# Splitting the attention scores of batches 2 and 3 into three fp32r products on a Trainium2 core

## The chip, the core and the metric

One kernel runs on one core of a Trainium2 chip. A core has five engines that run side by side and wait for each other through semaphores: TensorE (PE in the rows, with its weight loads as PEld), VectorE (DVE), ScalarE (ACT), GpSimd (POOL) and SyncE (SP, which here only issues DMAs). TensorE reads SBUF and writes PSUM, which has eight banks of 128 x 512 fp32. The metric is the device time of one execution in microseconds (us).

## The reference

Three stages follow each other. Inputs q, k, v are fp32 of shape (4 batches, 8 heads, 576 positions, 64 dims); f has one decay per position.

```python
scores = (q @ k.T) / sqrt(64) + (cum[i] - cum[j])      # cum = cumsum(log(f)), causal mask
attn   = softmax(scores);  a = attn @ v                # -> x, 2304 tokens x 512
h      = x @ w_in;  g = h * tanh(softplus(h));  z = g @ w_out      # 512 -> 2048 -> 512
out    = max(z @ w1, z @ w2, z @ w3) @ w_out2                      # 512 -> 768 -> 512
```

## The kernel before

All engines get one list of instructions each. The order of every list is set ahead of time by a scheduler, which takes the program as it is written, its priorities (attention is emitted at a high priority, the first feed-forward product `h` at a normal one) and its own estimate of durations. On the chip every engine then works through its list in that order.

**Attention** takes two heads at a time: 16 head pairs, 4 per batch, so batches 2 and 3 are the last eight. In this document "a pair" is such a pair of heads. For each pair `prep` turns q and k with TensorE transposes (`tr`) and ScalarE copies them from PSUM to SBUF as `qT` (128 x 512) and `kT` (128 x 576): head 0 of the pair on partitions 0 to 63 (`U`), head 1 on 64 to 127 (`L`). The last 64 query rows of both heads share one 128 x 128 operand `q4`, which holds head 0 in one quarter, head 1 in the opposite one and zeros elsewhere. `score_mm` (line 330) makes one product of scores. For query tiles 0 to 3 it contracts over 64 partitions, one head on each half of the array's rows, and writes the two heads to two different PSUM banks of the tile `sc`; the widths are 128 and 256 (together), 384, and 512. For the last query tile it contracts over all 128 partitions, twice 288 wide. All of these operands are fp32.

VectorE then adds the decay, masks and takes the row minimum (line 390), ScalarE takes the exponential (L396), VectorE the reciprocal of the sum, GpSimd scales the rows (L360), TensorE turns them back (`pp`, L429), ScalarE or VectorE copies them out, and TensorE multiplies with v (`av`, L415), here with the two heads on the two halves of the array's columns. The result is split into `xh` and `xl`, two fp32r parts, by `split` (L129).

The PSUM tiles `tr`, its companion `rest` (for the last 64 rows), and `pp` take turns in one pool of three banks.

**The first feed-forward product** `h = x @ w_in` runs beside it: its instructions fill TensorE between those of attention. It is already a split product: `mm3` (L179) sums `wh*xh + wh*xl + wl*xh` in PSUM, three fp32r products where high and low parts are rounded halves of the fp32 operands. `w_in` is loaded, converted and split during batches 0 and 1 (`load_w_in`; GpSimd does a clamp and the low half). Its staging pool is freed after the last piece.

After attention VectorE and ScalarE convert `w_out`; when `h` is done, `y` (the product with `w_out`) starts, and after it the last stage. Neither is touched by the change.

Of the kernel before, what the change touches and what calls it, by code (L numbers as in the profile page):

```python
# [9 lines left out]
F32 = mybir.dt.float32  # L10
F32R = mybir.dt.float32r
BF16 = mybir.dt.bfloat16
I32 = mybir.dt.int32
AF = mybir.ActivationFunctionType
ALU = mybir.AluOpType
# [17 lines left out]
BLK = 256  # L33
BLK2 = 512
LEAD = 2

# [28 lines left out]
def tile_decay_attention__mish_ff__max3_ff(  # L65
# [16 lines left out]
    nc = tc.nc  # L82
    B, H, S, D = q.shape
# [7 lines left out]
    scale = 1.0 / float(D) ** 0.5  # L91
# [10 lines left out]
    ident = const.tile([128, 128], F32, name="ident")  # L102
# [4 lines left out]
    with tc.tile_pool(name="setup", bufs=1) as sp:  # L107
# [3 lines left out]
            out=maskf, in_=maskf, pattern=[[-1, 128]], compare_op=ALU.is_ge,  # L111
# [64 lines left out]
    def queued(last):  # L176
        return tc.issue_after(last[-1].ins) if last else ExitStack()
# [14 lines left out]
    top = ExitStack()  # L192
# [31 lines left out]
    as_ = at.enter_context(tc.tile_pool(name="as", bufs=1, side="right"))  # L224
# [5 lines left out]
    def att_psum(name):  # L230
        return aps.tile([128, 512], F32, name=name, tag="ps", bufs=3)

    U, L = slice(0, 64), slice(64, 128)
# [5 lines left out]
    vs = [aw.tile([128, 640], F32, name=f"vs{i}") for i in range(3)]  # L239
# [6 lines left out]
    q4 = [as_.tile([128, 128], F32, name=f"q4_{i}") for i in range(2)]  # L246
    for t in q4:
        nc.gpsimd.memset(t, 0.0)
    for t in vs:
        nc.gpsimd.memset(t[U, 512:640], 0.0)  # L250
    count = dict(unit=0, bank=0, sc=0)

    def load(i, b, hp):

# [23 lines left out]
    def decay(J, h, qt):  # L278

        c2, c4 = J["cb"]  # L280
        if h is None:
            return c4.rearrange("p (a c) -> p a c", c=288)
        t = c2[:, h]
        if qt == 0:
            return t[:, 5:6, :]
        if qt == 1:
            return t[:, 0:7:6, :]
        if qt == 2:
            return t[:, 0:3, :].rearrange("p b c -> p (b c)")[:, None, :]
        return t[:, 0:6, :].rearrange("p (a b) c -> p a (b c)", a=2)[:, :, 0:256]  # L290
# [10 lines left out]
    def prep(J):  # L301

        b, hp, raw = J["b"], J["hp"], J["raw"]
        qq = as_.tile([128, 512], F32, name="qT", bufs=2)
        kk = as_.tile([128, S], F32, name="kT", bufs=2)
        last, v_ = q4[J["i"] % 2], vs[J["i"] % 3]
        rest = att_psum("tr")
        for i, dst in ((1, kk), (0, qq)):
            tr = att_psum("tr")
            with queued(last_av):  # L310
                for c in range(4):
                    nc.tensor.transpose(tr[:, c * 128:c * 128 + 128], raw[i][:, c * 128:c * 128 + 128], ident)
                last_tr[:] = [nc.tensor.transpose(rest[:, i * 64:i * 64 + 64], raw[i][U, 512:640], ident[U, U])]
            nc.scalar.activation(dst[:, 0:512], tr, AF.Copy)  # L314
        nc.scalar.activation(kk[:, 512:S], rest[:, 64:128], AF.Copy)
        for h, rows in enumerate((U, L)):
            nc.scalar.activation(last[rows, h * 64:h * 64 + 64], rest[rows, 0:64], AF.Copy)
        for h in range(2):
            nc.sync.dma_start(
                v_[:, h * 256:(h + 1) * 256].rearrange("p (t d) -> p t d", t=4),  # L320
                v[b, 2 * hp + h, 0:512, :].rearrange("(t p) d -> p t d", t=4),
            )
        nc.sync.dma_start(
            v_[L, 512:640].rearrange("p (h d) -> p h d", h=2),
            v[b, 2 * hp:2 * hp + 2, 512:S, :].rearrange("h p d -> p h d"),
        )
        J.update(q=qq, q4=last, k=kk, vs=v_)
        mask_decay(J)

    def score_mm(J, h, qt, dst, c0, w):  # L330
        if h is None:
            lhs, rows = J["q4"], slice(0, 128)
        else:
            rows = (U, L)[h]
            lhs = J["q"][rows, qt * 128:qt * 128 + 128]
        nc.tensor.matmul(dst, lhs, J["k"][rows, c0:c0 + w], start=True, stop=True, skip_group_check=True)  # L336

    def scores(J, g):


        P = {}
        u = count["unit"]
        count["unit"] += 1
        sm = sums[u % 4]
        mn = aw.tile([128, 6], F32, name="mn", bufs=4)
        rr = aw.tile([128, 5], F32, name="rr", bufs=4)
        tiles = [(h, qt) for qt in ((0, 1) if g == 0 else (2, 3)) for h in range(2)]
        if g == 1:
            tiles.append((None, 4))
        made = []  # L350
        col = 0

        def scale_rows(part):

            cs = slice(part[0], part[-1] + 1)
            with tc.high_priority(400):
                nc.vector.tensor_scalar(rr[:, cs], sm[:, cs], 1e-9, None, op0=ALU.add)
                nc.vector.reciprocal(rr[:, cs], rr[:, cs])  # L358
                for ci in part:
                    nc.gpsimd.tensor_scalar(made[ci], made[ci], rr[:, ci:ci + 1], 1.0, op0=ALU.mult, op1=ALU.mult)  # L360

        for ci, (h, qt) in enumerate(tiles):
            wd = (qt + 1) * 128 if qt < 4 else S
            Pt = aw.tile([128, wd], F32, name=f"P{qt}_{h}", bufs=LEAD)
            made.append(Pt)
            if h is None:
                P[4] = Pt
            else:
                P[h, qt] = Pt
            cb = decay(J, h, qt)  # L370
            if h is None:
                cb = [cb[:, n:n + 1] for n in range(2)]
            else:
                cb = [cb]
            s0 = 128 if qt == 1 else 0
            if not h and qt != 1:
                count["sc"] += 1
                pair = (aps if count["sc"] % 2 or not eps else eps[0]).tile([128, 2, 512], F32, name="sc", bufs=1)
                for n in range(2):
                    if h is None:  # L380
                        score_mm(J, h, qt, pair[:, n, :288], 288 * n, 288)
                    else:
                        score_mm(J, n, qt, pair[:, n, :wd], 0, wd)
                if qt == 0:
                    for n in range(2):
                        score_mm(J, n, 1, pair[:, n, 128:384], 0, 256)
            for pi, (c0, w) in enumerate([(0, wd)] if qt < 4 else [(0, 288), (288, 288)]):
                sc = pair[:, h or pi, s0:s0 + w]
                like = lambda t: t.rearrange("p (a c) -> p a c", a=cb[pi].shape[1])
                nc.vector.tensor_tensor_reduce(  # L390
                    out=like(Pt[:, c0:c0 + w]), in0=like(sc), in1=cb[pi],
                    scale=-scale, scalar=(3e38 if pi == 0 else mn[:, col - 1:col]),
                    op0=ALU.add, op1=ALU.min, accum_out=mn[:, col:col + 1],
                )
                col += 1
            nc.scalar.activation(  # L396
                Pt, Pt, AF.Exp, scale=-1.0, bias=mn[:, col - 1:col], accum_out=sm[:, ci:ci + 1],
            )
            if ci == 1:
                scale_rows([0, 1])  # L400
        scale_rows(list(range(2, len(tiles))))
        return P
# [49 lines left out]
    def attention():  # L452
# [9 lines left out]
        pend = []  # L462
        for n in range(len(units) + LEAD):
            if n == 6 + LEAD:
                eps.clear()
                early.close()
                eps_h.append(sa.enter_context(tc.tile_pool(name="hps", bufs=2, space=PSUM, reuse_waits="tile")))
            if n < len(units):
                ji, g = units[n]
                pend.append((J[ji], g, scores(J[ji], g)))  # L470
            if n >= LEAD:
                unit = pend.pop(0)
# [62 lines left out]
    while True:  # L535

        with tc.high_priority(AHEAD):
            done = next(attn, None)
        if done is None:
            break  # L540

        na += 1
        for _ in range(2 if 2 <= na <= 9 else na == 1):
            next(wgen, None)
        if len(loaded) == NFP and not x4:
            top.close()
            x4.append(top.enter_context(tc.tile_pool(name="x4", bufs=1)))
            x4[0].tile([128, 216], F32, name="gap")
        credit += RATE
        while credit >= 1.0:  # L550
            credit -= 1.0
            if next(steps, None) is None:
                credit = 0.0
# [113 lines left out]
    for step, (ib, fp, a) in enumerate(todo):  # L667
        n = blocks1[ib][1]
        if fp == 0 and a == 0:
            y = [yps.tile([128, n], F32, name=f"y{j}", tag="y") for j in range(KD)]  # L670
        parts = ahead.pop(0)
# [123 lines left out]
    hl = [hp0.tile([128, BLK2], F32R, name=f"hl0_{c}") for c in range(NF2)]  # L795
    sgen = sums_of_weights(smk)
    for ft in range(NF2):
        g = [gps[ft % 2].tile([128, BLK2], F32, name=f"g{m}") for m in range(3)]
        for m in range(3):
            for c in range(KD):  # L800
                w = wa[m][ft // 3, c // 2]
# [26 lines left out]
    for t0 in (BLK2, BLK2 + 2 * HALF):  # L828
        hh = [hp2.tile([128, 2 * HALF], F32R, name=f"hh{c}") for c in range(NF2)]
        hl = [hp2.tile([128, 2 * HALF], F32R, name=f"hl{c}") for c in range(NF2)]  # L830
        for p in range(3):
            fs = slice(p * 128, p * 128 + 128)
            for m in range(3):
                S = []
                for k in range(4):
                    t = sst.tile([128, 2, 2, 128], F32R, name="s")
# [49 lines left out]
            for i, eng in ((0, "pool"), (2, "dve"), (1, "dve"), (3, "dve")) if p == 2 else ((i, "pool") for i in range(4)):  # L886
                f, h = p + 3 * (i // 2), i % 2
# [37 lines left out]
```

## Time and profile before

| | |
|---|---|
| median of 3 runs | 909.84 us (909.51 to 910.46) |
| profiled execution | 909.78 us |
| its span from first to last instruction | 907.7 us, granted clock 0.992 of 2.4 GHz |
| TensorE busy | 882.8 us (97%) |
| VectorE / ScalarE / GpSimd busy | 497.1 / 400.7 / 232.7 us |

The time of an execution is its span and some 2 us around it. The busy time of TensorE counts every matmul from its start to a modelled end, and matmuls overlap; so what a matmul costs in a stream is read from one start to the next, not from its duration. fp32 matmuls show as two records each (two passes), fp32r matmuls as one.

### The profile page before, as it was taken

How to read it: one execution, taken by the hardware profiler on the slowest of the kernel's cores; microseconds unless marked ns; L12 is line 12 of the kernel's file. 1: busy time of each engine (PE TensorE's matmuls, PEld its weight loads, DVE VectorE, ACT ScalarE, POOL GpSimd, SP SyncE). 2: the span in 40 equal slices, each digit the busy share in tenths (PEclk: the TensorE clock that was granted, in tenths of full speed). 3: DMA queues.
4: the chain of work that ended last, by engine and by line, in shares of the span. 5: the costliest groups of instructions: out<-in, count | busy, mean ns of one | idle time of the engine just before them, and what ended most of it. 6: DMA issues, size and time to landing. Idle time of an engine off the chain costs nothing.

```text
span 907.7 us, 13930 instructions
## 1 busy us (share of the span) xinstructions
PE 882.8 (97%) x4800; PEld 704.8 (78%) x4800; DVE 497.1 (55%) x1186; ACT 400.7 (44%) x913; POOL 232.7 (26%) x317
## 2 busy tenths in 40 slices
PE   6898999999999999999999999999999999999998
PEld 3565666767767778889888888889888998889986
DVE  3598675344444343991367575775855447424440
ACT  4687666454443432533465545553433222412211
POOL 3689987222222220000020000000121332013310
PEclk8989999999999999999999999999999999999999
DMA  7896664444333115863456666663499444333401
GB/s 183 227 226 171 179 192 117 115 134 127 105 102 108 47 48 178 292 226 128 143 181 217 214 216 222 217 226 98 162 359 322 124 123 117 111 96 126 139 23 60
DMA packets 125030, 145.25 MB, mean 160 GB/s; under 512 B 64736, under 2 KB 78048, under 8 KB 124960
## 3 DMA queue, kind: packets, MB, share of 16 engines
q1 hardware_dynamic: 105856, 102.41, 39.0%
q10 hardware_dynamic: 16416, 27.79, 8.3%
q0 software_dynamic: 2688, 14.16, 4.3%
q8 instruction: 38, 0.62, 0.3%
q14 instruction: 32, 0.26, 0.1%
HBM read 102.83 MB, written 41.49 MB: 159 GB/s over the span
## 4 chain that ended last, share of the span: by engine, by line
PE 89%; POOL 3%; DMA 2%; DVE 2%; issue 1%; ACT 1%; SPq 1%; POOLq 0%
PE y L181 7%; PE y L183 7%; PE y L182 7%; PE h L181 7%; PE h L182 7%; PE h L183 7%; PE q L182 6%; PE q L183 6%; PE q L181 6%; PE sc L336 5%; PE av L415 5%; PE pp L429 5%; PE o L181 3%; PE o L182 3%; PE o L183 3%; PE g L181 2%
## 5 line engine op out<-in xcount | busy, mean ns | idle before, releaser
L181 PE MATMUL h<-xh,wi 128*128 128x512 f32 (+1 forms) x320 | 121.4, 380 | 1.6 <-ACT he L522 1.3
L182 PE MATMUL h<-xl,wi 128*128 128x512 f32 (+1 forms) x320 | 120.6, 377 | 1.8 <-DVE xl L137 1.8
L183 PE MATMUL h<-xh,wi 128*128 128x512 f32 (+1 forms) x320 | 120.7, 377 | 0.0
L182 PE MATMUL y<-gl,wo 128*128 128x512 f32 (+1 forms) x320 | 117.7, 368 | 0.0
L183 PE MATMUL y<-gh,wo 128*128 128x512 f32 (+1 forms) x320 | 117.6, 368 | 0.0
L181 PE MATMUL y<-gh,wo 128*128 128x512 f32 (+1 forms) x320 | 106.3, 368 | 0.0
L360 POOL TENSOR_SCALAR P<-P,rr 128x128 f32<-128x128 f32 (+3 forms) x128 | 74.0, 592 | 87.5 <-DVE rr L358 31.5
L659 DVE TENSOR_TENSOR gl<-g,gh 128x512 fp32r<-128x512 f32 x72 | 50.0, 697 | 83.3 <-ACT gh L658 83.1
L396 ACT ACTIVATE P<-P,mn 128x128 f32<-128x128 f32 (+3 forms) x128 | 70.7, 554 | 53.4 <-DVE mn L390 50.2
L652 ACT ACTIVATE g<-g 128x512 f32<-128x512 f32 x72 | 45.2, 632 | 70.6 <-DMA g<-h_d 65.7
L181 PEld LDWEIGHTS h<-xh,wi 128*128 128x128 f32 x320 | 60.1, 188 | 14.6 <-issue 2.2
L182 PEld LDWEIGHTS h<-xl,wi 128*128 128x128 f32 x320 | 60.1, 188 | 14.0 <-issue 2.8
L183 PEld LDWEIGHTS h<-xh,wi 128*128 128x128 f32 x320 | 60.3, 188 | 11.5 <-issue 2.7
L182 PEld LDWEIGHTS y<-gl,wo 128*128 128x128 f32 x320 | 60.3, 188 | 10.2
L183 PEld LDWEIGHTS y<-gh,wo 128*128 128x128 f32 x320 | 60.2, 188 | 10.1
L181 PEld LDWEIGHTS y<-gh,wo 128*128 128x128 f32 x320 | 60.3, 189 | 10.1
L522 ACT ACTIVATE he<-h 128x512 f32<-128x512 f32 x56 | 33.3, 595 | 57.0 <-PE h L183 52.4
L851 DVE TENSOR_TENSOR u<-q,p 128x448 f32<-128x448 f32 x36 | 22.4, 621 | 62.3 <-PE q L183 60.7
L336 PE MATMUL sc<-kT,qT 64*128 64x128 f32 (+3 forms) x256 | 51.9, 500 | 3.6 <-DVE mn L390 3.3
L429 PE MATMUL pp<-ident,P 128*128 128x128 f32 x320 | 51.1, 285 | 4.0 <-ACT qT L314 3.6
L658 ACT ACTIVATE gh<-g 128x512 fp32r<-128x512 f32 x72 | 45.0, 627 | 22.0 <-PE y L183 20.9
L429 PEld LDWEIGHTS pp<-ident,P 128*128 128x128 f32 x320 | 37.0, 143 | 20.1 <-issue 5.0
(141 smaller groups left out, 1850.3 us busy)
## 6 DMA issues: line engine op xcount, KB each, us to landing
g<-h_d SPq DMA_DIRECT2D x72, 256.0 KB, 2.9
s<-s_d SPq DMA_DIRECT2D x72, 256.0 KB, 3.0
h_d<-he ACTq DMA_DIRECT2D x56, 256.0 KB, 2.9
wr<-in_moe_w_out_dram SPq DMA_DIRECT2D x22, 512.0 KB, 4.6
wr<-in_moe_w_dram SPq DMA_DIRECT2D x24, 384.0 KB, 3.8
s_d<-sk POOLq DMA_DIRECT2D x12, 768.0 KB, 5.8
cb<-cum_d SPq DMA_DIRECT2D x32, 256.0 KB, 4.2
wr<-in_moe_w_in_dram SPq DMA_DIRECT2D x16, 512.0 KB, 4.5
```

What stands on the lines that cost most here:

```text
L181: nc.tensor.matmul(ps, wh, xh, start=start, stop=False, skip_group_check=True)
L182: nc.tensor.matmul(ps, wh, xl, start=False, stop=False, skip_group_check=True)
L183: return nc.tensor.matmul(ps, wl, xh, start=False, stop=stop, skip_group_check=True)
L336: nc.tensor.matmul(dst, lhs, J["k"][rows, c0:c0 + w], start=True, stop=True, skip_group_check=True)
L360: nc.gpsimd.tensor_scalar(made[ci], made[ci], rr[:, ci:ci + 1], 1.0, op0=ALU.mult, op1=ALU.mult)
L396: nc.scalar.activation(Pt, Pt, AF.Exp, scale=-1.0, bias=mn[:, col - 1:col], accum_out=sm[:, ci:ci + 1],)
L415: last = nc.tensor.matmul(acc[(U, L)[h], off:off + w], J["vs"][:, n * 64:n * 64 + 64], T[:, at[h]:at[h] + w], start=kt == 0 and off == 0, ...
L429: turn = nc.tensor.transpose(pp[:, n * 128:n * 128 + 128], Pt[:, k0:k0 + 128], ident)
L522: nc.scalar.activation(he, h, AF.Copy)
L652: nc.scalar.activation(g, g, AF.Mish)
L658: on_act[:] = [nc.scalar.activation(gh, g, AF.Copy)]
L659: on_dve[:] = [nc.vector.tensor_tensor(out=gl, in0=g, in1=gh, op=ALU.subtract)]
```

## The change

For batches 2 and 3 (`SPLIT_FROM = 2`) q and k are no longer kept as fp32 operands. `prep` now writes `qT`, `kT` and the last rows' operand as fp32r high parts (ScalarE's copy, which rounds) and VectorE subtracts that from the PSUM value to make the low parts `ql`, `kl` and `q4l`. `score_mm` gets a list of products (head 0 and head 1, or the two 288-wide pieces) and makes three terms `q*k`, `q*kl`, `ql*k`, each term of one head directly followed by the same term of the other. The low parts and the two `q4` pairs live in a pool `low` that takes memory of the freed staging pool of `w_in`; ScalarE writes zeros to the `q4` tiles there once.

```diff
@@ prep
-        qq = as_.tile([128, 512], F32, name="qT", bufs=2)
-        kk = as_.tile([128, S], F32, name="kT", bufs=2)
+        parts = b >= SPLIT_FROM
+        kind = F32R if parts else F32
+        qq = as_.tile([128, 512], kind, name="qT", bufs=2)
+        kk = as_.tile([128, S], kind, name="kT", bufs=2)
         last, v_ = q4[J["i"] % 2], vs[J["i"] % 3]
+        if parts:
+            ql = lowp[0].tile([128, 512], F32R, name="ql", bufs=2)
+            kl = lowp[0].tile([128, S], F32R, name="kl", bufs=2)
+            last = q4r[J["i"] % 2]
+            low = {id(qq): ql, id(kk): kl}
+
+        def put(dst, lo, src):
+            nc.scalar.activation(dst, src, AF.Copy)
+            if parts:
+                nc.vector.tensor_tensor(out=lo, in0=src, in1=dst, op=ALU.subtract)
+
...
-            nc.scalar.activation(dst[:, 0:512], tr, AF.Copy)
-        nc.scalar.activation(kk[:, 512:S], rest[:, 64:128], AF.Copy)
+            put(dst[:, 0:512], low[id(dst)][:, 0:512] if parts else None, tr)
+        put(kk[:, 512:S], kl[:, 512:S] if parts else None, rest[:, 64:128])
...
+                put(last[0][rows, cs], last[1][rows, cs], rest[rows, 0:64])
...
-    def score_mm(J, h, qt, dst, c0, w):
-        if h is None:
-            lhs, rows = J["q4"], slice(0, 128)
-        else:
-            rows = (U, L)[h]
-            lhs = J["q"][rows, qt * 128:qt * 128 + 128]
-        nc.tensor.matmul(dst, lhs, J["k"][rows, c0:c0 + w], start=True, stop=True, skip_group_check=True)
+    def score_mm(J, jobs):
+
+        terms = [(0, 0), (0, 1), (1, 0)] if len(J["q"]) == 2 else [(0, 0)]
+        for ti, (a, c) in enumerate(terms):
+            for h, qt, dst, c0, w in jobs:
+                if h is None:
+                    lhs, rows = J["q4"][a], slice(0, 128)
+                else:
+                    rows = (U, L)[h]
+                    lhs = J["q"][a][rows, qt * 128:qt * 128 + 128]
+                nc.tensor.matmul(
+                    dst, lhs, J["k"][c][rows, c0:c0 + w], start=ti == 0, stop=ti == len(terms) - 1,
+                    skip_group_check=True,
+                )
...
+            lowp.append(top.enter_context(tc.tile_pool(name="low", bufs=1)))
+            for i in range(2):
+                q4r.append([lowp[0].tile([128, 128], F32R, name=f"q4{n}{i}") for n in "hl"])
+                for t in q4r[i]:
+                    nc.scalar.activation(t, ident, AF.Copy, scale=0.0)
```

The scheduler lays out every engine's list anew. On TensorE, where the second pair of batch 2 is scored against 512 keys, the list before has (sc is the score tile, kT and qT its operands, `x2` two instructions in a row, here the two heads):

```order
L182 MATMUL h<-xl_447,wi_154 128x512
L183 MATMUL h<-xh_446,wi_154 128x512
L181 MATMUL h<-xh_446,wi_154 128x512
L336 MATMUL sc<-kT,qT 128x512 x2
L182 MATMUL h<-xl_447,wi_154 128x512
```

and the changed kernel, at a product of the same kind:

```order
L456 MATMUL pp<-ident,P_1_2152 128x128
L456 MATMUL pp<-ident,P_1_2169 128x128
L362 MATMUL sc<-kT,qT 128x512 x2
L362 MATMUL sc<-kl,qT 128x512 x2
L362 MATMUL sc<-kT,ql 128x512 x2
L182 MATMUL h<-xh_589,wi_149 128x512
```

Two instructions became six, head by head in turn, and they still stand together. Where the first pair of batch 2 is scored, TensorE's list had

```order
L181 MATMUL h<-xh_446,wi_153 128x512
L336 MATMUL sc<-kT,qT 128x128 x2
L336 MATMUL sc<-kT,qT 128x256 x2
L415 MATMUL av<-TB,vs_179 64x128 x2
L415 MATMUL av<-TB,vs_179 64x64 x10
L429 MATMUL pp<-ident,P_0_1759 128x128
```

and has now

```order
L362 MATMUL sc<-kT,qT 128x128 x2
L362 MATMUL sc<-kl,qT 128x128 x2
L362 MATMUL sc<-kT,ql 128x128 x2
L456 MATMUL pp<-ident,P_None 128x128
L362 MATMUL sc<-kT,qT 128x256
L456 MATMUL pp<-ident,P_None 128x128
L362 MATMUL sc<-kT,qT 128x256
L362 MATMUL sc<-kl,qT 128x256
L456 MATMUL pp<-ident,P_None 128x128
L362 MATMUL sc<-kl,qT 128x256
L456 MATMUL pp<-ident,P_None 128x128
L362 MATMUL sc<-kT,ql 128x256
```

Here five transposes `pp` stand between the terms, and the two heads of a term no longer follow each other. On VectorE, ahead of the first pair of batch 2, the changed list has (each row ends with the engines it waits for)

```order
L417 ISA P_1_1905,mn<-sc,cb 128x512
L417 ISA mn 128x1
L138 TENSOR_TENSOR xl_590<-av,xh_589 128x256 [waits Activation_49]
L320 TENSOR_TENSOR kl<-tr,kT 128x512 [waits Pool_49]
L320 TENSOR_TENSOR ql<-tr,qT 128x512
L320 TENSOR_TENSOR kl<-tr,kT 128x64
L320 TENSOR_TENSOR q4l_1064<-tr,q4h_1063 64x64 [waits Activation_49] x2
```

The five subtractions (L320) are new; the first of them waits for GpSimd, whose memory the pool `low` takes over.

## Rows read from the trace of the kernel before

**Rows 1.** Windows: busy us (x instructions) of each engine, clock, DMA share, GB/s.
```profile
75.00:100.00 25.00, 21.50 (x154) 15.01 (x152) 20.82 (x56) 17.81 (x51) 22.82 (x25) 1.00 0.76 210
100.00:125.00 25.00, 22.47 (x141) 15.70 (x137) 16.71 (x45) 14.91 (x39) 23.53 (x22) 1.00 0.64 182
125.00:150.00 25.00, 23.63 (x153) 16.24 (x155) 19.55 (x50) 16.68 (x44) 21.04 (x22) 1.00 0.47 135
...
153.26:354.40 201.14, 201.14 (x1303) 144.59 (x1302) 82.30 (x297) 88.25 (x258) 49.88 (x98) 1.00 0.33 98
```
**Rows 2.** TensorE timeline, batches 2 and 3: start, duration, instructions, matmul records.
```profile
232.32 0.40 PE L182 MATMUL h<-xl,wi 128*128 128x512 f32 x1
232.65 1.13 PE L336 MATMUL sc<-kT,qT 64*128 64x512 f32 x4
233.71 0.50 PE L183 MATMUL h<-xh,wi 128*128 128x512 f32 x1
234.05 0.40 PE L181 MATMUL h<-xh,wi 128*128 128x512 f32 x1
234.28 0.39 PE L182 MATMUL h<-xl,wi 128*128 128x512 f32 x1
...
238.08 1.24 PE L336 MATMUL sc<-kT,q 128*128 128x288 f32 x4
239.24 0.45 PE L415 MATMUL av<-TB,vs 128*64 128x64 f32 x6
...
244.32 0.93 PE L336 MATMUL sc<-kT,qT 64*128 64x128 f32 x8
245.18 0.49 PE L183 MATMUL h<-xh,wi 128*128 128x512 f32 x1
...
250.44 0.92 PE L336 MATMUL sc<-kT,qT 64*128 64x384 f32 x4
251.28 0.66 PE L429 MATMUL pp<-ident,P 128*128 128x128 f32 x4
251.70 0.48 PE L183 MATMUL h<-xh,wi 128*128 128x512 f32 x1
```
**Rows 3.** TensorE timeline, two 256-wide fp32r products at the end of h.
```profile
420.25 0.28 PE L183 MATMUL h<-xh,wi 128*128 128x256 f32 x1
420.37 0.28 PE L181 MATMUL h<-xh,wi 128*128 128x256 f32 x1
```
**Rows 4.** TensorE timeline, the last av of attention between two products of h.
```profile
353.07 0.39 PE L181 MATMUL h<-xh,wi 128*128 128x512 f32 x1
353.39 1.02 PE L415 MATMUL av<-TB,vs 128*64 128x128 f32 x24
354.34 0.50 PE L182 MATMUL h<-xl,wi 128*128 128x512 f32 x1
354.67 0.40 PE L183 MATMUL h<-xh,wi 128*128 128x512 f32 x1
```
**Rows 5.** TensorE timeline in batch 1, a 384-wide score whose heads stand apart.
```profile
106.83 0.88 PE L336 MATMUL sc<-kT,qT 64*128 64x384 f32 x2 [2.00 <-DVE mn L390]
107.64 0.33 PE L415 MATMUL av<-TB,vs 128*64 128x64 f32 x2
107.90 0.91 PE L336 MATMUL sc<-kT,qT 64*128 64x384 f32 x2
```
**Rows 6.** Waits of TensorE from 75 to 152 us: total, times, longest.
```profile
PE sc L336 <- DVE mn L390: 3.3, 2, 2.0
```
**Rows 7.** Lines by shape up to 420 us: busy us, mean ns, idle before, releasers.
```profile
L582 DVE TENSOR_TENSOR wo<-wt,wo 128x512 fp32r<-128x512 f32 x16 | 11.0, 688 | 4.7 <-ACT wo L579 4.6
L137 DVE TENSOR_TENSOR xl<-av,xh 128x64 fp32r<-128x64 f32 x8 | 1.7, 218 | 4.5 <-ACT xh L131 4.5
L314 ACT ACTIVATE kT<-tr 128x512 f32<-128x512 f32 x16 | 9.5, 592 | 4.7 <-PE tr L312 4.7
```
**Rows 8.** GpSimd timeline, its last two pieces of w_in.
```profile
144.20 2.96 POOL L137 TENSOR_TENSOR wi<-wt,wi 128x512 fp32r<-128x512 f32 x2
```

More of the change, by code (lines that the diff above doesn't have):

```diff
@@ L35 @@
 LEAD = 2
+SPLIT_FROM = 2
 def turned_layout(g):
@@ L251, in tile_decay_attention__mish_ff__max3_ff @@
     count = dict(unit=0, bank=0, sc=0)
+    lowp, q4r = [], []
     def load(i, b, hp):
@@ L313, in prep @@
                 last_tr[:] = [nc.tensor.transpose(rest[:, i * 64:i * 64 + 64], raw[i][U, 512:640], ident[U, U])]
-            nc.scalar.activation(dst[:, 0:512], tr, AF.Copy)
-        nc.scalar.activation(kk[:, 512:S], rest[:, 64:128], AF.Copy)
+            put(dst[:, 0:512], low[id(dst)][:, 0:512] if parts else None, tr)
+        put(kk[:, 512:S], kl[:, 512:S] if parts else None, rest[:, 64:128])
         for h, rows in enumerate((U, L)):
-            nc.scalar.activation(last[rows, h * 64:h * 64 + 64], rest[rows, 0:64], AF.Copy)
+            cs = slice(h * 64, h * 64 + 64)
+            if parts:
+                put(last[0][rows, cs], last[1][rows, cs], rest[rows, 0:64])
+            else:
+                put(last[rows, cs], None, rest[rows, 0:64])
         for h in range(2):
@@ L326, in prep @@
         )
-        J.update(q=qq, q4=last, k=kk, vs=v_)
+        if parts:
+            J.update(q=(qq, ql), q4=last, k=(kk, kl), vs=v_)
+        else:
+            J.update(q=(qq,), q4=(last,), k=(kk,), vs=v_)
         mask_decay(J)
-    def score_mm(J, h, qt, dst, c0, w):
-        if h is None:
-            lhs, rows = J["q4"], slice(0, 128)
-        else:
-            rows = (U, L)[h]
-            lhs = J["q"][rows, qt * 128:qt * 128 + 128]
-        nc.tensor.matmul(dst, lhs, J["k"][rows, c0:c0 + w], start=True, stop=True, skip_group_check=True)
+    def score_mm(J, jobs):
[4 more added lines that the diff above has]
+                    lhs, rows = J["q4"][a], slice(0, 128)
+                else:
+                    rows = (U, L)[h]
[4 more added lines that the diff above has]
+                )
     def scores(J, g):
@@ L378, in scores @@
                 pair = (aps if count["sc"] % 2 or not eps else eps[0]).tile([128, 2, 512], F32, name="sc", bufs=1)
[L379 to L383, printed above, removed]
+                if h is None:
+                    score_mm(J, [(h, qt, pair[:, n, :288], 288 * n, 288) for n in range(2)])
+                else:
+                    score_mm(J, [(n, qt, pair[:, n, :wd], 0, wd) for n in range(2)])
                 if qt == 0:
-                    for n in range(2):
-                        score_mm(J, n, 1, pair[:, n, 128:384], 0, 256)
+                    score_mm(J, [(n, 1, pair[:, n, 128:384], 0, 256) for n in range(2)])
             for pi, (c0, w) in enumerate([(0, wd)] if qt < 4 else [(0, 288), (288, 288)]):
```

## The prediction, made before the changed kernel ran

> **What bounds the kernel now.** I read the windows first, then TensorE's timeline, then its waits. In batches 2 and 3, from the first score at 153.26 us to the end of the last av at 354.40, TensorE is busy 201.14 of 201.14 us at the full granted clock of 1.00, while VectorE is busy 82.30, ScalarE 88.25 and GpSimd 49.88 [rows 1]. So there every ns taken from TensorE's list is a ns gained, and every ns added is lost; `h` fills whatever attention leaves. Before batch 2 it is different: from 75 to 150 us TensorE is idle 3.50 + 2.53 + 1.37 = 7.4 us, and GpSimd is busy 22.8, 23.5 and 21.0 of each 25 us [rows 1]; the largest wait of TensorE there is of scores for a PSUM tile that VectorE still reads, 3.3 us in two waits [rows 6]. Extra work of TensorE can fall into these holes.
>
> **What a score costs now.** A product of one width is two heads of two records each. From start to next start the 512-wide one takes 233.71 - 232.65 = 1.06 us, the 384-wide one 251.28 - 250.44 = 0.84, the 128- and 256-wide ones together 245.18 - 244.32 = 0.86 [rows 2]. The first two differ by 0.22 us over 128 columns, 1.7 ns per column, four periods of 2.4 GHz. One 288-wide product on the whole array, with the same two passes, also takes about four periods per column (below). Two heads in turn would take eight, so the heads run at the same time on the two halves of the rows. What is left, 1.06 - 512 x 1.7 ns, is 0.19 us of fixed cost. The pair of 288-wide products on the whole array takes 239.24 - 238.08 = 1.16 us, of which I put 0.20 to entry and exit [rows 2], so 0.96 for four passes.
>
> **What three terms cost.** An fp32r product of `h` takes 0.23 us per 512 columns (234.05 to 234.28) [rows 2] and 0.12 per 256 (420.25 to 420.37) [rows 3]: 0.43 ns per column and some 0.01 fixed. That gives 0.175 for 384 and 0.133 for 288; for 128 the line would give 0.067, and the nearest row of that width, four fp32 transposes, 0.42 us or 0.105 each (251.28 to 251.70) [rows 2]. I take 0.105, because a new weight load goes with each product there as well. If the two heads overlap as they do in fp32, per pair of heads:
> 128 and 256: 0.19 + 3 x 0.105 + 3 x 0.12 = 0.865 against 0.86, nothing;
> 384: 0.19 + 3 x 0.175 = 0.715 against 0.84, -0.125;
> 512: 0.19 + 3 x 0.23 = 0.88 against 1.06, -0.18;
> 288 twice: 6 x 0.133 = 0.80 against 0.96, -0.16.
> Together -0.46 us, for eight pairs of heads **-3.7 us**. Bounds: with 0.067 for the 128-wide terms -0.58, or -4.6 in all; if each head pays the fixed 0.01 to 0.015 for itself (twelve times more), -0.30 or -2.4.
>
> For the 128-wide terms, rows leave 0.067 to 0.12 open. The Trainium skill (TensorE: Matmul & The Clock Gate, LDWEIGHTS) puts a weight load at its columns over 1.2 GHz, so 107 ns for 128 columns; by that the terms cannot be shorter than the transposes' 0.105 and the sum is -3.7, without it -4.6.
>
> **What the new order costs.** In the timeline h before a score starts 0.33 us ahead of it where 0.23 would do (232.32 to 232.65), h after it takes 0.34 (233.71 to 234.05), and the score has its 0.19 [rows 2]: 0.40 us for going to half rows and back, 0.20 per change. Around av, h takes 0.32 before (353.07 to 353.39) and 0.33 after (354.34 to 354.67) [rows 4]: at least 0.10 per change. The Trainium skill (TensorEngine Tiling (Array Packing), Key Properties) says that a change of tiling mode drains the engine, and the trace agrees, with 0.10 to 0.20 us each; the rule speaks against a list that scatters the terms.
> I counted changes between whole array, half rows and half columns in the two lists of TensorE. From the first score of batch 2 to the last av there were 120 and are 130: 34 against 13 up to the second pair's first score, 96 against 107 behind it. Ten more at 0.12 to 0.20 is +1.2 to +2.0; I take **+1.7**, as most are around scores.
> Heads that no longer follow each other run one after the other: one head's 384 columns take 0.81 us (106.83 to 107.64) [rows 5], as much as both together [rows 2]. In the first pair of batch 2 the 256- and 384-wide terms need five intervals where three would do: 2 x 0.12 + 2 x 0.175 = 0.59; two later 384-wide terms are parted by a transpose, up to 0.175 each, and I take 0.2 for both. **+0.8.** Three 256-wide av products stand alone behind it, too, at 256 x 1.7 ns = 0.43 each: **+1.3.**
> Before batch 2 there are 113 changes for 106 (+1.1) and one 512-wide score of batch 1 with its heads apart (512 x 1.7 ns = +0.87), so 2.0 us more, and the list has 13 more products of h there (3.0 us), while 1.8 us of av and transposes moved behind the mark: 3.2 us more work in a stretch with 7.4 idle. If the idle time takes all of it, the net is 2.0 - 3.2 = -1.2; if none, +2.0. I take the middle, **+0.4**.
>
> **VectorE, ScalarE, memory.** Per pair VectorE gets two subtractions of 128 x 512 (0.69 each by the same operation on fp32r outputs), one of 64 columns (0.22) and two of 64 x 64 (I take 0.22 too) [rows 7]: 2.0 us, 16 us for eight pairs, on an engine busy 82 of 201 us. TensorE's h covers this. What is less covered: the banks of `tr` and `rest` come free only after VectorE's subtraction behind ScalarE's 0.59 us copy [rows 7], and `pp` waits for the same three banks. Behind a waiting `pp` stand h, scores and av, since TensorE's list is in order. The first subtraction waits for GpSimd's last split of w_in, which ended at 144.20 + 2.96 = 147.16 [rows 8], 6 us before the first score of batch 2; behind it on VectorE stand the last tile's minimum of the previous pair and two copies of `pp`. ScalarE's four zero fills wait for it as well. From 0 to +3 us; I take **+0.5**. No DMA is added; those of q, k and the decay move by a few places among SP's issues and land ahead of their use by a unit of work.
>
> **Sum:** -3.7 + 1.7 + 0.8 + 1.3 + 0.4 + 0.5 = +1.0 on the profiled execution's 909.78 us, which stands at the median of the runs (909.84): **910.8 us**. The stages behind h are unchanged and start as much later. The likeliest case's own range, 909.0 to 912.2, comes from the bounds of the 128-wide terms and of the stretch before batch 2.
>
> **Rivals.**
> The gain shows: the holes before batch 2 take the extra 3.2 us and shrink further since VectorE's two waits [rows 6] fall away in the new order. Then that term is -1.2 - 3.3 = -4.5 in place of +0.4, and the time 905.9; with one of the two waits gone 907.5. For it speaks that GpSimd, and not TensorE, is the busiest engine there, and that the list has h to fill with; against it, that nothing in the change touches what makes these holes.
> Slower by waits: the subtraction holds the transposes' banks. If each pair delays TensorE by one subtraction, 0.69 x 8 = 5.5 us in place of 0.5, 915.8. It decides once VectorE reaches a subtraction later than TensorE reaches the third bank user behind it. Against it: TensorE waits for nothing in 201 us now [rows 1], with VectorE busy 41%, and would be at 49%.
> The change doesn't do what it says: heads of an fp32r term take turns. Per pair 6 x (0.105 + 0.12 + 0.175 + 0.23) + 0.57 = 4.35 against 2.76, +1.59, less 0.16 for the 288s: +1.43, +11.4 for eight instead of -3.7, without the +0.8 for parted heads: 910.8 + 14.3 = 925. Every fp32r product of before uses whole rows, so no row excludes it; the overlap of fp32 heads speaks against it.
>
> **Chances.** About 0.2% (1.8 us) is what a measurement of this kernel can tell from no change. Forecast 0.55: 0.43 within it, 0.10 slower, 0.02 faster. Gain shows 0.17: 0.14 faster, 0.03 the same. Waits 0.20, all slower. Heads in turn 0.08, all slower. So faster 0.16, same 0.46, slower 0.38. Range: 907 cuts off about half of the gain's case, 916.5 some of the waits' and all of the heads in turn: 907 to 916.5.
>
> **What would show it.** In the profile after: start to start about 0.88 us for a 512-wide score, 0.72 for 384, 0.87 for 128 and 256, and second heads some ns behind the first. If these are 1.5 us and more, heads take turns. If the last av of attention ends some 6 us later than 354.40 though fewer products of h are left behind it (21 fewer, 4.8 us), the order costs what I say. Idle time of TensorE with a subtraction (L320) as releaser between 150 and 360 us would make the waits right, and idle well under 7.4 us between 75 and 150 the gain.

## The result

The changed kernel takes **915.52 us** (median of 4 runs, 915.08 to 917.69) against 910.15 for the kernel before in the same session (909.51 to 910.56): a ratio of 1.0064 (of the means), 95% interval 1.0047 to 1.0082. It is 5.4 us slower. The forecast was 910.8, no change; the time lies within the range of 907 to 916.5, but the likeliest case did not come, and the side with a chance of 0.38 did.

Busy time of the engines (share of the span) and instructions, from the page of the changed kernel:

```profile
PE 888.6 (97%) x4880; PEld 715.9 (78%) x4880; DVE 511.0 (56%) x1226; ACT 402.9 (44%) x917; POOL 232.3 (25%) x317
```

TensorE is busy 5.8 us longer, and the span is 913.2 for 907.7. The windows of the changed kernel, the last of them from batch 2's first score to the start of the last av, 0.2 us short of the stretch in [rows 1], with the same columns:

```profile
75.00:100.00 25.00, 21.51 (x140) 14.08 (x139) 18.67 (x53) 16.65 (x48) 22.56 (x25) 0.93 0.73 202
100.00:125.00 25.00, 25.00 (x148) 17.44 (x149) 16.75 (x45) 15.52 (x41) 21.96 (x20) 1.00 0.64 183
125.00:150.00 25.00, 22.05 (x127) 15.22 (x126) 19.01 (x48) 14.04 (x39) 21.88 (x21) 0.93 0.39 114
...
157.69:363.10 205.41, 205.41 (x1405) 155.77 (x1406) 96.38 (x334) 89.89 (x259) 50.06 (x98) 1.00 0.32 97
```

TensorE still never waits in batches 2 and 3 (205.41 of 205.41 us), although VectorE has 14 us more to do there. Ahead of them the granted clock, 1.00 in all three windows of [rows 1], is 0.93 in two.

**Where the 5.5 us of the span went.** I cut both traces at 75 us, at batch 2's first score, at the start of the last av and at the first `y`. The last three come at 153.3, 354.2 and 424.3 us before, and at 157.7, 363.1 and 430.2 after. Products of `h` moved over the cuts (124, 426 and 398 in the three stretches before; 137, 434 and 377 after), so I took from each stretch the same fixed price for every product of `h`, transpose and av in it (0.23 us per 512-wide `h`, 0.11 per transpose). What is left is scores, changes of the array's layout, waits and a lower clock:

| stretch | length before, after | without its `h`, transposes and av | difference |
|---|---|---|---|
| 75 us to batch 2's first score | 78.3, 82.7 | 27.8, 31.1 | **+3.3** |
| to the last av: the scores in it | 200.9, 205.4 (both) | 30.2, 29.0 | **-1.2** |
| to the last av: the rest | | 17.7, 19.7 | **+2.1** |
| to the first `y` | 70.1, 67.1 | 0.2, 2.0 | **+1.8** |

Behind the first `y` the changed kernel is 0.35 us shorter (482.97 for 483.32). The rounded sum is +5.6.

**The scores.** TensorE's timeline of the changed kernel (start, duration, instructions): a 512-wide score with its terms together, and then the first pair of batch 2.

```profile
313.20 0.50 PE L362 MATMUL sc<-kT,qT 64*128 64x512 f32 x2
313.55 0.40 PE L362 MATMUL sc<-kl,qT 64*128 64x512 f32 x2
313.78 0.39 PE L362 MATMUL sc<-kT,ql 64*128 64x512 f32 x2
314.10 0.66 PE L456 MATMUL pp<-ident,P 128*128 128x128 f32 x4
```

```profile
157.69 0.33 PE L362 MATMUL sc<-kT,qT 64*128 64x128 f32 x2
157.85 0.27 PE L362 MATMUL sc<-kl,qT 64*128 64x128 f32 x2
157.96 0.27 PE L362 MATMUL sc<-kT,ql 64*128 64x128 f32 x2
158.17 0.33 PE L456 MATMUL pp<-ident,P_None 128*128 128x128 f32 x1
158.43 0.38 PE L362 MATMUL sc<-kT,qT 64*128 64x256 f32 x1
158.74 0.33 PE L456 MATMUL pp<-ident,P_None 128*128 128x128 f32 x1
159.00 0.38 PE L362 MATMUL sc<-kT,qT 64*128 64x256 f32 x1
159.00 0.38 PE L362 MATMUL sc<-kl,qT 64*128 64x256 f32 x1
159.32 0.33 PE L456 MATMUL pp<-ident,P_None 128*128 128x128 f32 x1
```

Both heads' terms stand in one row (`x2`), and the next row starts 0.23 to 0.35 us later: 314.10 - 313.20 = 0.90 us for six fp32r products, where [rows 2] have 1.06 for four records, two fp32 products of two passes each. The 128-wide terms start 0.16 and 0.11 us apart and end 0.21 later. The Trainium skill (TensorE: Matmul & The Clock Gate, LDWEIGHTS) puts a weight load of 128 columns at 107 ns; the shortest of these steps, 0.11, agrees. In the second fence a transpose stands behind each 256-wide term but one (two of them start together at 159.00). Such a term takes 0.31 to 0.32 us to the next start, instead of 0.12 in a row, and a lone transpose 0.25 to 0.27 instead of 0.11.

**Ahead of batch 2** two places account for nearly all of the 3.3 us. First the kernel before, TensorE's timeline (in brackets idle time and what ended it):

```profile
85.13 0.92 PE L336 MATMUL sc<-kT,qT 64*128 64x384 f32 x4 [1.25 <-DVE mn L390]
...
87.04 2.31 PE L415 MATMUL av<-TB,vs 128*64 128x256 f32 x36
89.29 1.13 PE L336 MATMUL sc<-kT,qT 64*128 64x512 f32 x4
...
131.00 0.60 PE L312 MATMUL tr<-ident,rawk 128*128 128x128 f32 x4
131.36 0.48 PE L181 MATMUL h<-xh,wi 128*128 128x512 f32 x1
...
133.18 0.92 PE L336 MATMUL sc<-kT,qT 64*128 64x384 f32 x4
134.02 0.50 PE L182 MATMUL h<-xl,wi 128*128 128x512 f32 x1
```

The same places in the changed kernel:

```profile
85.43 0.92 PE L362 MATMUL sc<-kT,qT 64*128 64x384 f32 x4 [1.79 <-DVE mn L417]
...
87.02 3.96 PE L442 MATMUL av<-TB,vs 128*64 128x256 f32 x36
90.92 1.13 PE L362 MATMUL sc<-kT,qT 64*128 64x512 f32 x4
...
133.45 0.60 PE L327 MATMUL tr<-ident,rawk 128*128 128x128 f32 x4
136.66 0.92 PE L362 MATMUL sc<-kT,qT 64*128 64x384 f32 x4 [2.61 <-DVE mn L417]
...
138.39 0.63 PE L183 MATMUL h<-xl,wi 128*128 128x512 f32 x1
138.82 0.63 PE L184 MATMUL h<-xh,wi 128*128 128x512 f32 x1
```

The same 36 av records take 90.92 - 87.02 = 3.90 us where they took 2.25, at a granted clock of 0.50 from 87.0 to 90.4 us. Products of `h` start 0.43 us apart instead of 0.23 from 138.39 to 141.38, again at a granted clock of 0.50; that is the 1.2 GHz level instead of 2.4. The first costs 1.65 us, the second 7 x 0.2 plus a little, 1.6. Both come after TensorE stood for VectorE's minimum `mn`, 1.79 and 2.61 us. The reason of the longer of these stands is the list: before, seven products of `h` stand between the transposes `tr` at 131.00 and the score at 133.18, and fill the wait wholly. Now they stand behind the score. The idle time as a whole did not grow: 6.4 us from 75 us to batch 2's first score against 7.4. The two lower-clock stretches (3.25), the 512-wide scores there, one of them with its heads apart (4.2 us to the next starts for 3.2, so 1.0), and 1.0 less idle make 3.25 of the 3.3.

**Behind attention** TensorE waits twice for ScalarE's copies `he`. The waits of TensorE from 355 to 425 us, and the timeline of ScalarE and TensorE at the longer one:

```profile
PE h L182 <- ACT he L549: 0.9, 2, 0.7
```

```profile
371.59 1.28 ACT L684 ACT_TABLE_LOAD   x1
372.88 0.63 ACT L684 ACTIVATE g<-g 128x512 f32<-128x512 f32 x1
372.99 0.39 PE L184 MATMUL h<-xh,wi 128*128 128x512 f32 x1
373.42 0.58 ACT L549 ACTIVATE he<-h 128x512 f32<-128x512 f32 x1
...
374.05 0.50 PE L182 MATMUL h<-xh,wi 128*128 128x512 f32 x1 [0.67 <-ACT he L549]
```

The copy stands behind a table load and the first activation of `g`; the next product starts 1.06 us after the one before it instead of 0.23. With 0.62 us at 367.02 and 0.46 at 376.67 for the same step, and 0.1 more at the step behind each, that is the stretch's 1.8.

### The profile page after: what moved, and what is told of

Same layout as the page of the kernel before. It is cut to its first block, busy times and chain, and to the rows that moved or that the text cites. A ratio compares the mean times of both kernels' runs of the same rounds, so it can differ in the third digit from the quotient of the medians.

```text
span 913.2 us, 14131 instructions
## 1 busy us (share of the span) xinstructions
PE 888.6 (97%) x4880; PEld 715.9 (78%) x4880; DVE 511.0 (56%) x1226; ACT 402.9 (44%) x917; POOL 232.3 (25%) x317
## 4 chain that ended last, share of the span: by engine, by line
PE 90%; DMA 2%; DVE 2%; issue 1%; POOL 1%; ACT 1%; SPq 1%; POOLq 0%; ACTq 0%; DVEq 0%
PE y L182 7%; PE y L184 7%; PE y L183 7%; PE h L182 7%; PE h L183 7%; PE h L184 7%; PE sc L362 6%; PE q L183 6%; PE q L184 6%; PE q L182 6%; PE av L442 5%; PE pp L456 5%; PE o L182 3%; PE o L183 3%; PE o L184 3%; PE g L182 2%
## 5 line engine op out<-in xcount | busy, mean ns | idle before, releaser
L684 ACT ACTIVATE g<-g 128x512 f32<-128x512 f32 x72 | 45.4, 633 | 70.1 <-DMA g<-h_d 66.6
L442 PE MATMUL av<-TB,vs 128*64 128x64 f32 (+2 forms) x576 | 50.5, 295 | 0.7 <-ACT TB L462 0.3
```

The lines of the kernel that those rows point to most:

```text
L442: last = nc.tensor.matmul(acc[(U, L)[h], off:off + w], J["vs"][:, n * 64:n * 64 + 64], T[:, at[h]:at[h] + w], start=kt == 0 and off == 0, ...
L684: nc.scalar.activation(g, g, AF.Mish)
```

## The experiments

Each was timed on one chip with the kernel before. The columns are median time, ratio to the kernel before with its interval, and the three differences against the kernel before that the table above has for the changed one (each from the one profiled execution).

| kernel | us | ratio (95%) | ahead of batch 2 | batches 2, 3 | behind |
|---|---|---|---|---|---|
| the change | 915.52 | 1.0064 (1.0047 to 1.0082) | +3.3 | +0.9 | +1.8 |
| e1 terms together | 908.77 | 0.9989 (0.9980 to 0.9998) | +4.8 | -4.1 | 0 |
| e2 fills late | 912.07 | 1.0024 (1.0015 to 1.0033) | +0.4 | +2.7 | +0.5 |
| e3 both | 904.90 | 0.9948 (0.9936 to 0.9960) | +2.7 | -6.5 | +0.9 |
| e4 subtractions only | 912.27 | 1.0034 (1.0020 to 1.0047) | +0.5 | +1.7 | +0.2 |
| e5 head by head | 906.16 | 0.9956 (0.9939 to 0.9973) | +3.1 | -6.5 | +2.0 |
| e6 e4, together | 913.53 | 1.0034 (1.0022 to 1.0046) | +2.6 | +0.2 | +0.6 |
| e7 no subtraction | 904.77 | 0.9945 (0.9933 to 0.9957) | +1.1 | -4.9 | -0.1 |
| e8 fills only | 913.88 | 1.0037 (1.0024 to 1.0050) | +5.6 | 0 | 0 |
| e9 fills on GpSimd | 914.75 | 1.0046 (1.0032 to 1.0060) | +0.6 | +0.6 | +0.6 |
| e10 tail copies | 904.40 | 0.9947 (0.9929 to 0.9965) | +0.8 | -6.5 | +0.4 |

The stretch ahead of batch 2 varies from execution to execution. TensorE's list up to batch 2's first score is one and the same in e2, e3, e4, e5, e6 and e10, and the column has +0.4 to +3.1 for it; so a single entry says little, and what the fills cost is read from the medians. The profiled executions of e1, e3, e5 and e8 (910.87, 906.89, 908.01 and 915.85 us) had the longest times of their runs, those of the changed kernel and of e9 (915.08 and 910.92) the shortest. Every edited kernel's trace has one or two stretches at the lower clock between 75 us and batch 2's first score; the one trace of the kernel before has none, and whether its other executions do is not known.

**e1: are the scattered terms the loss?** The matmuls of the three terms get a higher priority, so that the scheduler leaves nothing between them. The list up to batch 2 stays that of the changed kernel.

```diff
-                nc.tensor.matmul(
+                with tc.high_priority(400) if len(terms) > 1 else ExitStack():
+                    nc.tensor.matmul(
```

> The changed kernel with a higher priority for the split terms alone, so that the six instructions of a product stand together in TensorE's list; lists up to batch 2's first score are the same as in the changed kernel (113 changes of array mode, 149 products of h), behind it 13 + 99 changes in place of 34 + 96. Theory 1 (the terms gain 3.6 us, the new lists lose 9): 18 changes at 0.12 to 0.20 us (2.2 to 3.6) and some 0.6 to 1.0 us of heads apart come back: 911.0 to 912.8. Theory 2 (VectorE's subtractions and the banks they hold delay TensorE): the subtractions are all there, so 915 to 916.

It came to 908.77, 6.7 us below the changed kernel and lower than either theory had it. Scores of batches 2 and 3 take 26.3 us of TensorE (30.2 before, 29.0 in the change), the rest 17.5. The changes between whole array, half rows and half columns number 113 (131 in the change), counted on the trace. The slower stretch ahead of batch 2, whose list is the same, is still there.

**e2: are the zero fills the loss ahead of batch 2?** The four fills of the `q4` tiles move from the place where the pool opens into `prep` of batch 2's first two pairs.

```diff
@@ prep
             last = q4r[J["i"] % 2]
+            if b == SPLIT_FROM and hp < 2:
+                for t in last:
+                    nc.scalar.activation(t, ident, AF.Copy, scale=0.0)
@@ the pool "low"
-                for t in q4r[i]:
-                    nc.scalar.activation(t, ident, AF.Copy, scale=0.0)
```

> The changed kernel with ScalarE's zero fills moved into the preparation of batch 2's first two pairs; before batch 2's first score TensorE's list has 106 changes and 142 products of h, as in the kernel before 106 and 136, behind it 35 + 99. Theory 1: what is lost ahead of batch 2 (its first score came 4.4 us later, of which 3.0 were 13 more products of h) goes down by the seven changes and the wait of 2.6 us with its clock drop: 911 to 914. Theory 2: 915 to 916, since all subtractions are there.

912.07, as the first theory had it: the median is 3.5 us below the changed kernel's, the +3.3 ahead of batch 2 becomes +0.4, and the waits for `mn` are back at 3.2 us in two. Batches 2 and 3 have +2.7 here instead of +0.9, with 135 changes and a rest of 21.5 us. Four more changes do not account for that. Part of it is the clock, which fell once in this trace behind batch 2's first score. The window from 150 to 175 us, with the columns of [rows 1]:

```profile
150.00:175.00 25.00, 25.00 (x137) 16.43 (x136) 9.21 (x35) 9.56 (x28) 5.18 (x10) 0.93 0.30 85
```

TensorE is busy throughout it, the granted clock is 0.93, and the twelve av records behind the first pair's scores take 2.76 us where the changed kernel's take 1.45. With the product of `h` behind them that is 1.6 us; what is left, +1.1, is near the changed kernel's +0.9. TensorE's last wait, of 1.3 us, had ended at 144.66, 11 us ahead of this fall.

**e3: both edits.**

> Both edits: terms together and fills late; 106 changes before batch 2, 12 + 89 behind it, 207 in all against 226 in the kernel before. Theory 1: the scores' gain of 3.6 us and 19 changes fewer at 0.12 to 0.20 (2.3 to 3.8 us) show: 902.5 to 906.5 (faster than before). Theory 2: the subtractions cost what they cost: 912 or more.

904.90, as the first theory had it, and faster than both kernels. The late fills are worth 3.9 us here (908.77 in e1). TensorE's timeline of e3 at the first pair of batch 2:

```profile
155.76 0.33 PE L366 MATMUL sc<-kT,qT 64*128 64x128 f32 x2
155.92 0.28 PE L366 MATMUL sc<-kl,qT 64*128 64x128 f32 x2
156.03 0.27 PE L366 MATMUL sc<-kT,ql 64*128 64x128 f32 x2
156.15 0.33 PE L366 MATMUL sc<-kT,qT 64*128 64x256 f32 x2
156.32 0.28 PE L366 MATMUL sc<-kl,qT 64*128 64x256 f32 x2
156.43 0.28 PE L366 MATMUL sc<-kT,ql 64*128 64x256 f32 x2
156.64 0.44 PE L460 MATMUL pp<-ident,P 128*128 128x128 f32 x2
```

The two products together take 156.64 - 155.76 = 0.88 us; in the changed kernel they and five transposes take 161.02 - 157.69 = 3.33. In all, the scores of eight pairs take 26.1 us, **4.1 less than before**, at 102 changes and a rest of 15.3.

**e4 and e6: do the subtractions cost?** e4 keeps the fp32 scores and lets VectorE make `ql`, `kl` and `q4l` for nothing. e6 gives e4's scores the priority of e1.

```diff
-                put(last[0][rows, cs], last[1][rows, cs], rest[rows, 0:64])
+            put(last[rows, cs], l4[rows, cs] if parts else None, rest[rows, 0:64])
...
-        J.update(q=(qq, ql), q4=last, k=(kk, kl), vs=v_)
+        J.update(q=qq, q4=last, k=kk, vs=v_)
```

> The kernel before (fp32 scores) with the eight pairs' subtractions made on VectorE and not used, no zero fills; 106 changes before batch 2, 12 + 104 behind it, 222 in all against 226. Theory 1: no gain and no loss to speak of, 908.5 to 911.5. Theory 2: the subtractions alone cost 4 us or more: 914 or more.

912.27, between the theories. TensorE waits for nothing in batches 2 and 3 here either. The loss there (+1.7) goes with the list: in three of the eight 384-wide scores the heads no longer follow each other, as here (timeline of e4):

```profile
158.74 0.91 PE L351 MATMUL sc<-kT,qT 64*128 64x384 f32 x2
...
160.41 0.91 PE L351 MATMUL sc<-kT,qT 64*128 64x384 f32 x2
```

Two rows of one head each, 0.9 us apiece, in place of one row `x4` of 0.84; all eight cost 9.3 us for 6.7, which is more than the +1.7.

> e4_subtract_only with a higher priority for the fp32 scores of batches 2 and 3, so that the two heads of a product stand together (in e4 three 384-wide products had theirs apart, and its 384-wide scores took 9.3 us against 6.7 in the kernel before). The subtractions are all made. Theory 1 (order): 2.6 us come back, 908.5 to 910.5. Theory 2 (subtractions delay): 912 to 913 as e4.

913.53, above both theories and by its ratio the same as e4. The 384-wide scores are back at 6.8 us, and batches 2 and 3 at +0.2, but the time did not follow. Ahead of batch 2 the trace has a wait of 1.9 us for ScalarE's copy `he`, and a granted clock of 0.93 from 100 to 150 us. TensorE's list there is that of e4 (+0.5) and of e3 (+2.7), so this does not come from a new list, and no run shows where e6's 3.4 us go.

**e5: do the heads have to take turns in the program?** In e3 the loops over terms and heads are exchanged, so that TensorE's list has three terms of head 0 and then three of head 1. The lists of the other engines stay.

```diff
-        for ti, (a, c) in enumerate(terms):
-            for h, qt, dst, c0, w in jobs:
+        for h, qt, dst, c0, w in jobs:
+            for ti, (a, c) in enumerate(terms):
```

> e3_both with the loops of terms and heads exchanged: all three terms of one head, then all three of the other; the lists of all other engines are the same, and TensorE's differs only within the six instructions of a product. If the heads overlap only when they follow each other term by term, a product takes five intervals in place of three: per pair of heads 2 x (0.107 + 0.12 + 0.175 + 0.23) = 1.26 us, for eight 10.1, so 913 to 916. If TensorE runs the second head's terms ahead of the first's, 904 to 906, as e3_both (904.9).

906.16, not told apart from e3 by their intervals. The timeline of e5 shows why (`x2` here is one term of both heads, although three products stand between them in the list):

```profile
254.56 0.51 PE L366 MATMUL sc<-kT,qT 64*128 64x512 f32 x2
254.90 0.40 PE L366 MATMUL sc<-kl,qT 64*128 64x512 f32 x2
255.14 0.39 PE L366 MATMUL sc<-kT,ql 64*128 64x512 f32 x2
```

Head 1's first term starts 10 ns behind head 0's first, and ahead of head 0's second. That is the second case of the expectation.

**e7: the subtractions taken out of e3.** The low parts are filled once with zeros instead.

```diff
             nc.scalar.activation(dst, src, AF.Copy)
-            if parts:
-                nc.vector.tensor_tensor(out=lo, in0=src, in1=dst, op=ALU.subtract)
```

> e3_both without the subtractions: the low parts are set to zero once, the 12 terms per pair of heads that use them are still made, so the output lacks their share. TensorE's list has 109 + 13 + 99 changes (221) against 207 in e3. Theory 1: VectorE's subtractions cost nothing by themselves, and 14 changes more at 0.15 us make it 905 to 908. Theory 2: 8 subtraction groups less, 899 to 903.

904.77 against e3's 904.90, just below what the first theory had: 16 us of VectorE's work for eight pairs cost nothing that shows. The two lists are not the same: e7 has 113 changes in batches 2 and 3 for e3's 102, and is 1.6 us slower there, as 11 changes at some 0.15 us make it. Ahead of batch 2 its trace is 1.6 us shorter, which lies within what one list shows from execution to execution; so a cost of the subtractions of up to some 2 us in all is not excluded by the times, but TensorE waits for nothing in batches 2 and 3 in either trace.

**e8: the fills alone.** The kernel before, with the pool `low` and the four fills, and no split.

```diff
             x4[0].tile([128, 216], F32, name="gap")
+            lowp.append(top.enter_context(tc.tile_pool(name="low", bufs=1)))
+            for i in range(2):
+                q4r.append([lowp[0].tile([128, 128], F32R, name=f"q4{n}{i}") for n in "hl"])
+                for t in q4r[i]:
+                    nc.scalar.activation(t, ident, AF.Copy, scale=0.0)
```

> The kernel before with the pool and ScalarE's four zero fills at the place where the change puts them, and nothing else; the split is not made. Theory 1: the fills alone move the lists (115 + 13 + 107 = 235 changes against 226): 910.5 to 913. Theory 2: four copies of a quarter us on an engine that is busy 44%: as the kernel before, 909 to 910.5.

913.88, more than the first theory's 913: four instructions that nothing reads cost 3.8 us. In the trace, the longest of seven executions, it is 5.6 us, all of it ahead of batch 2's first score (158.9 us for 153.3). Behind it TensorE's list is that of the kernel before but for three more products of `h`, and its durations are the same. The timeline of e8 at the score that we know from 136.66:

```profile
137.94 1.65 PE L337 MATMUL sc<-kT,qT 64*128 64x384 f32 x4 [2.60 <-DVE mn L391]
139.53 0.80 PE L182 MATMUL h<-xl,wi 128*128 128x512 f32 x1
140.12 0.63 PE L183 MATMUL h<-xh,wi 128*128 128x512 f32 x1
```

The same wait of 2.6 us, and the lower clock behind it. The fills themselves run from 150.63 to 151.54, some 13 us later. So this wait comes from the list that the scheduler makes with them, and not from ScalarE standing at them; e9 tests that.

**e9: the fills on GpSimd,** in otherwise nearly the same lists.

```diff
-                    nc.scalar.activation(t, ident, AF.Copy, scale=0.0)
+                    nc.gpsimd.memset(t.bitcast(F32), 0.0)
```

> The changed kernel with the four zero fills on GpSimd (memset) instead of ScalarE; the list of TensorE up to batch 2 differs in two neighbouring swaps, VectorE's not at all. Theory 1: it is the moved order of the work ahead of batch 2, not ScalarE standing at the fills, that costs there: batch 2's first score again at 156.5 to 159 us, time 913.5 to 917. Theory 2: the fills hold ScalarE back, and behind it the products of h: without them first score at 153 to 155.5, time 911 to 913.

914.75, as the moved order has it (the first theory); but the first score of the profiled execution is at 154.8, as the second has it. That execution had the shortest time of ten (910.92 to 917.12). Its timeline:

```profile
131.82 0.60 PE L327 MATMUL tr<-ident,rawk 128*128 128x128 f32 x4
135.01 0.92 PE L362 MATMUL sc<-kT,qT 64*128 64x384 f32 x4 [2.59 <-DVE mn L417]
135.86 0.50 PE L183 MATMUL h<-xl,wi 128*128 128x512 f32 x1
136.20 0.40 PE L184 MATMUL h<-xh,wi 128*128 128x512 f32 x1
136.44 0.40 PE L182 MATMUL h<-xh,wi 128*128 128x512 f32 x1
```

The same order of instructions, the same 2.6 us of idle time, and here the clock stays: `h` goes on at 0.23 to 0.24 us, and the granted clock is 1.00 from 125 to 150 us. At the first place, from 75 to 100 us, it is 0.93 as in the changed kernel. The wait comes from the list (the change, e1, e8 and e9 have it, 2.59 to 2.61 us each time, and no other trace has), the fall of the clock behind it only in some executions. That the longer executions of e9 had the fall is likely and not shown, since only one was profiled.

**e10: odd copies of `h` behind attention on VectorE,** in e3.

```diff
-            if j % 2 and done < NT and i:
+            if j % 2 and i:
```

> The kernel with terms kept together and fills late (904.9), with every odd copy of h behind attention's end on VectorE too, where ScalarE did all of them. TensorE's list is the same. Theory 1: waits of h for ScalarE's copies behind attention (1.0 to 2 us in the tail) go, time 903.3 to 904.5. Theory 2: VectorE's splits of w_in and w_out, which then stand behind copies, are late by as much, time 904.7 to 907.

904.40 against 904.90, with overlapping intervals: not told apart. The stretch from the last av to the first `y` went from 66.2 to 65.8 us; e3 already has only 0.2 us of TensorE's waits for `he` there, as e10 has, so there was little to gain. TensorE's list is the same in both, yet ahead of batch 2 their traces differ by 1.9 us.

## Why the prediction was right in its range and wrong in its terms

That 915.52 lies within 907 to 916.5 is luck. Its upper end was drawn to take in most of the rival of VectorE's waits, and these did not come; the time got there by three terms that came out 1.8 to 2.9 us higher than forecast. By the prediction's own terms, predicted and measured in us:

| term | predicted | measured |
|---|---|---|
| scores as three terms, together | -3.7 | -4.1 (e3) |
| heads and terms apart | +0.8 | +2.9 (29.0 less 26.1) |
| more changes, lone av | +3.0 | +2.1 |
| waits in batches 2 and 3 | +0.5 | 0 |
| ahead of batch 2 | +0.4 (-1.2 to +2.0) | +3.3 |
| the end of `h` | 0 | +1.8 |
| behind it | 0 | -0.4 |

**The scores were right.** The heads do overlap in fp32r, the prices of the widths hold within 0.02 us where the terms stand together (0.88 us for 128 and 256, 0.72 for 384, 0.89 to 0.90 for 512), and the gain appears when the list lets it. The rival of heads in turn falls.

**The order cost what was feared, in other shares.** Together the second and third term measure 5.0 us against 3.8. I priced a parted 256- or 384-wide term at what one more interval costs (0.12, 0.175); the changed kernel's rows give 0.31 and 0.37. A reason that fits is that each brings its own way into half rows and out; I had counted those changes in the other term. So the parting of the heads was too low by 2.1 us and the changes too high by 0.9. That the parting costs is shown by e1 and e3, where the same products stand together and their time falls from 29.0 to 26.3 and 26.1 us. The last av ended 8.9 us later than before, not some 6.

**The step that failed is "before batch 2".** I set the extra work of that stretch against its idle time as if that were one pool, and took the middle. What decided was where single instructions moved: seven products of `h` that had covered a wait for `mn` went behind it. And I gave the clock no term at all: [rows 1] show 1.00 in every window, with waits of 2.0 us in them [rows 6], so I took it as fixed. +3.3 is outside my bounds. That the fills bring it about is shown by three pairs of medians: 3.8 us for the fills alone (e8 over the kernel before), 3.5 for their later place in the changed kernel (e2), 3.9 with the terms together (e3 over e1). The clock's part in it (3.25 us) is read from one trace of the changed kernel, and in e9's trace one of its two places kept the full clock; how much of the median it makes is not shown.

**The end of `h` was left out.** "The stages behind h are unchanged and start as much later" overlooked that `h` itself reaches 21 products less far past attention, and that ScalarE's work on `w_out` and `g` then meets its copies of `h`. In the kernel before TensorE has no wait there. The fewer products alone do not make it: e3, e6, e9 and e10 have the same 377 there and lose 0.4 to 0.9 us, e5 has them and loses 2.0. e3 and e5 differ only in the order of terms, so part of this varies from execution to execution.

**The rival of VectorE's waits fell,** though its 915.8 lies next to the measured time: the changed kernel's trace has not one wait of TensorE between 150 and 350 us, and e7 without subtractions takes what e3 does. The right number there would have had a wrong reason. "The gain shows" came true for another list only (e3, 904.9; I had 905.9), and not by the holes ahead of batch 2 but by the terms that stand together.

**Open** is what makes the clock fall after one wait of 2.6 us and not after another of the same length, and in e2 with no wait near it, and why e4 and e6 lose 2.4 and 3.4 us: the parted heads of e4 are put right in e6, which is no faster.

## What to carry to other kernels

Where a scheduler lays out the lists, an instruction costs by what it moves, not only by what it takes: four fills of 0.3 us cost 3.8 us without any reader. So look in the new list at each place where an engine waited and see what stands ahead of the wait now. Price a product by its neighbours: products that share an array layout belong together, and a priority that keeps them so was worth 6.7 us here, 2.7 of it in the scores' own time (29.0 to 26.3). When a stretch has idle time on TensorE, count the stretches at the lower clock, and time such a kernel in several runs before trusting one trace of it: one list up to batch 2 gave +0.4 to +3.1 us in six traces.

## What the hardware showed that I had not expected

**The two halves of the rows overlap whatever the order of the list.** In e5 three terms of head 0 stand ahead of three of head 1, and the records still start in pairs, 2 to 10 ns apart. The Trainium skill (TensorE: Matmul & The Clock Gate, The mechanism) says that matmuls start and end strictly in the order of the program. This trace differs: head 1's first term starts at 254.57 us, head 0's second at 254.90. The measurement decides, and the time agrees with it (906.16 us, where heads one after the other would have made it 913 or more).

**A change of the array's layout costs some 0.15 us on the whole.** The rest of batches 2 and 3, without scores, is 15.3 us at 102 changes (e3), 17.7 at 121 (before), 19.7 at 131 (the change): 0.15 each in all three. This is an estimate: the level of the rest hangs on the fixed prices taken off before it, and the differences alone give 0.13 (before over e3) and 0.20 (the change over before). That the engine drains at such a change is also what the Trainium skill says (TensorEngine Tiling (Array Packing), Key Properties); a size comes from these rows.

**A wait can cost again behind it.** After 2.61 us of idle time `h` ran at the 1.2 GHz level for 3 us, 1.6 us of loss; after 2.59 us in e9 it did not. In e2 1.6 us went the same way in a stretch where TensorE was busy throughout.
